# Padding TensorE's program with 95 small matmuls, and loading two rows of wo over ten DMA engines

## The chip, the cores and the metric

One core of a Trainium2 chip. Times are device microseconds of one execution of the whole kernel; a profile's span is a little shorter than the time (244.6 against 246.1 us for the kernel before). The ratios below compare fast runs of the same chip and the same rounds; e5 to e8 are single runs, taken for their traces, and their state is not known.

The names used below: PE is TensorE, the matrix engine; DVE copies and reduces; SyncE (SP) issues the loads; SBUF is the on-chip memory, which the kernel addresses as 128 partitions. The profile counts sixteen DMA engines; they carry a load in packets. A semaphore is a counter that the reader of the data waits on. The queues q1 and q8 are those of the big loads and of PE's program.

## The reference

Two attention layers decode one token each; their outputs are concatenated. Layer A looks at the last 2048 positions of its cache, B at all 8192.

```python
# B, S=1, D=576; Hq=32, Hkv=16, Sk=8192, Dh=128; all bfloat16
def ref(x, k_cache, v_cache, wq, wo, W):             # W = 2048 for A, 8192 for B
    q = (x @ wq).reshape(B, 1, Hq, Dh).transpose(0, 2, 1, 3)
    k = repeat(k_cache[:, :, Sk - W:], 2, axis=1)    # each kv head serves two query heads
    v = repeat(v_cache[:, :, Sk - W:], 2, axis=1)
    p = softmax(einsum("bhqd,bhkd->bhqk", q, k) * Dh ** -0.5)
    o = einsum("bhqk,bhkd->bhqd", p, v)
    return o.transpose(0, 2, 1, 3).reshape(B, 1, Hq * Dh) @ wo
```

The inputs that are read come to 102.76 MB, and each byte is used once.

## The kernel before

Each operation is recorded with what it reads and writes; semaphores and waits follow from that. All big loads are issued by SyncE into one region of SBUF called `slots`. A loop runs five times on TensorE (once for A, four times for B): transposes of K, scores, softmax, sums over V. Then comes wo. Partition p holds rows 32p to 32p + 31 of wo, so "row j" below means 128 rows of wo, one on each partition, 1152 bytes a partition.

```python
    def load(dst, src, writes, dma):
        add("sp", lambda sp: sp.dma_start(dst, src()), writes=writes, dma=dma)
    ...
    def load_wo(P, lo, n, off, res):
        load(slots[:, off:off + n * DM], lambda: wos[P].rearrange("(p j) n -> p (j n)", p=128)[:, lo * DM:(lo + n) * DM],
             res, "wo%d_%d" % (P, lo))

    def wo_part(P, lo, n, off, res):                 # four matmuls a row of B
        ...
    wo_loads = [                                     # layer, first row, rows, place, what must be free
        (0, 0, 32, 0, [("k", 0), ("k", 1, 0)]),
        (1, 0, 21, WQ_W, [("k", 1, 1)]),
        (1, 21, 7, 2 * SLOT, [("v", 0), ("v", 1)]),
        (1, 28, 3, 2 * SLOT + 7 * DM, [("w", 0)]),
        (1, 31, 1, 2 * SLOT + 10 * DM, [("w", 1)])]
    for P, lo, n, off, res in wo_loads:
        load_wo(P, lo, n, off, res)
    combine([NG - 1])                                # the attention output of the last group
    o_columns(1)
    for P in range(2):
        for Q, lo, n, off, res in wo_loads:
            if Q == P:
                wo_part(P, lo, n, off, res)
        finish_out(P)                                # copy, then the output's DMA
```

## Time and profile before

| | before |
|---|---|
| time | 246.02 us (245.89 to 246.11, 3 runs) |
| span of the profile | 244.6 us |
| loads on q1 | 102.76 MB, 98.1% of sixteen engines' span |
| fetches of PE's program (q8) | 6 packets of 16,384 bytes |
| last landing of wo of B, row 31 | 242.24 us |
| copy of the result starts | 242.59 us |

The page and the chain are shown in the prediction. Two readings need more than the page gives. A load over all 128 partitions steps its semaphore sixteen times (row 31 from 240.25 to 242.24 us). I take each step as one DMA engine's, so the sixteen times in the trace's semaphore records tell how far apart the engines are; "last" is what a waiting engine sees (row 31's last step at 242.24, PE's last four matmuls from 242.29). And each packet of a transfer has a start and a length. Packets follow end to start (most often the next one starts 3 or 4 ns before the recorded end), so in a busy stretch they can be chained into sixteen rows, which I take for the engines, with a few packets ambiguous where two rows meet. In the kernel before each of the sixteen rows has eight of the 128 packets of 24,192 bytes.

### The profile page before, as it was taken

Reading aid. Unit: us, or ns where it says so; the run is one execution under the profiler, and the core shown is the slowest. Engines: PE = TensorE matmul, PEld = TensorE weight load, DVE = VectorE, ACT = ScalarE, POOL = GpSimd, SP = SyncE. Lnnn points to the kernel's source line nnn. Section 1 sums busy time; section 2 is a strip of 40 time slices with the busy share of each in tenths; the row PEclk is TensorE's granted clock in tenths of the full one; section 3 lists DMA queues with packets and bytes.
Section 4 is the critical chain, followed back from the end, with each engine's and each line's share of the span. In section 5 each row is a group of like instructions: output and inputs, shape, how many; then the busy total and the mean of one; then the engine's idle time right before and its main releaser. Section 6 shows DMA issues by size and latency. Waiting matters only on the chain. (4 is left out here: it accounts for less than half of the span.)

```text
span 244.6 us, 5211 instructions
## 1 busy us (share of the span) xinstructions
PE 165.4 (68%) x2325; PEld 121.3 (50%) x2325; DVE 88.2 (36%) x152; ACT 92.7 (38%) x95; POOL 6.3 (3%) x33
## 2 busy tenths in 40 slices
PE   0007339968389995393999362999457799945965
PEld 0002139746236773233887221987232787624854
DVE  0001407864316454203556302455322246543031
ACT  2000016855306686102678300687600378630000
POOL 5000100000000000000000000000000000000000
PEclk9999957997759999569899859799957589975599
DMA  9999999999999999899999999999989999989993
GB/s 338 434 410 418 434 437 426 429 426 426 445 426 430 482 407 450 380 439 429 478 439 429 413 418 429 434 504 397 461 375 434 429 488 397 461 388 428 414 409 135
DMA packets 4068, 102.88 MB, mean 421 GB/s; under 512 B 602, under 2 KB 732, under 8 KB 988
## 3 DMA queue, kind: packets, MB, share of 16 engines
q1 hardware_dynamic: 3900, 102.76, 98.1%
q8 instruction: 6, 0.10, 0.2%
q10 hardware_dynamic: 160, 0.00, 0.0%
q14 instruction: 2, 0.02, 0.0%
HBM read 102.76 MB, written 0.00 MB: 420 GB/s over the span
## 5 line engine op out<-in xcount | busy, mean ns | idle before, releaser
L506 ACT ACTIVATE kt<-ktps 128x1024 bf16<-128x1024 bf16 x80 | 79.5, 1036 | 89.6 <-PE ktps L496 89.6
L496 PE MATMUL ktps<-ident,slots 128*128 128x128 bf16 x1280 | 87.8, 234 | 22.5 <-PEq L214 19.2
L496 PEld LDWEIGHTS ktps<-ident,slots 128*128 128x128 bf16 x1280 | 81.7, 106 | 38.0 <-issue 37.9
L509 DVE COPY kt<-ktps 128x1024 bf16<-128x1024 bf16 x80 | 60.7, 768 | 59.0 <-PE ktps L496 59.0
L588 PE MATMUL opsum<-slots,ptm 128*32 128x512 bf16 x320 | 28.5, 532 | 9.8 <-PEq L214 9.8
L521 PE MATMUL sacc<-kt,qst 128*32 128x512 bf16 x320 | 25.4, 392 | 2.2 <-PEq L214 2.2
L588 PEld LDWEIGHTS opsum<-slots,ptm 128*32 128x32 bf16 x320 | 14.0, 129 | 22.9 <-issue 20.6
L559 PE MATMUL misc<-ident,psb 128*128 128x128 bf16 x40 | 4.6, 285 | 15.8 <-PEq L214 15.8
L547 ACT ACTIVATE psb<-sacc,stat 128x2048 bf16<-128x2048 f32 x5 | 9.8, 1967 | 10.1 <-DVE stat L536 10.1
L606 DVE TENSOR_TENSOR vtmp<-opsum,maskV 128x512 f32<-128x512 f32 x4 | 2.8, 692 | 30.2 <-PE opsum L588 30.2
L559 PEld LDWEIGHTS misc<-ident,psb 128*128 128x128 bf16 x40 | 3.4, 125 | 18.2 <-issue 18.2
L438 PE MATMUL misc<-xnine,twice 64*128 64x18 bf16 x1 | 0.2, 170 | 18.0 <-DMA xnine<-in_B_x_dram 18.0
L566 DVE TENSOR_TENSOR ptm<-misc,maskP 128x1024 bf16<-128x1024 bf16 x5 | 3.5, 691 | 16.0 <-PE misc L559 16.0
L521 PEld LDWEIGHTS sacc<-kt,qst 128*32 128x32 bf16 x320 | 5.0, 94 | 8.3 <-issue 4.6
L438 PEld LDWEIGHTS misc<-xnine,twice 64*128 64x128 bf16 x1 | 0.1, 99 | 18.0 <-issue 18.0
L462 ACT ACTIVATE qrow<-opsum 128x512 bf16<-128x512 f32 x1 | 0.6, 597 | 19.4 <-PE opsum L456 19.4
L690 PE MATMUL ktps<-slots,opj 128*32 128x144 bf16 (+1 forms) x192 | 6.7, 247 | 0.7 <-issue 0.5
L690 PEld LDWEIGHTS ktps<-slots,opj 128*32 128x32 bf16 x192 | 5.3, 96 | 1.9 <-issue 0.6
L447 DVE TENSOR_SCALAR xpad<-misc,par 128x5 bf16<-128x5 f32 (+1 forms) x8 | 1.2, 229 | 13.8 <-PE misc L438 13.8
L481 POOL COPY qst<-qcol 128x32 bf16<-128x32 bf16 x8 | 1.7, 211 | 147.4 <-PE sacc L521 147.4
L559 PE MATMUL turned<-ident,psb 128*128 128x128 bf16 x40 | 5.3, 313 | 0.0
L534 DVE TENSOR_REDUCE stat<-sacc 128x1 f32<-128x512 f32 x5 | 3.5, 691 | 4.4 <-PE sacc L521 4.4
(75 smaller groups left out, 52.9 us busy)
## 6 DMA issues: line engine op xcount, KB each, us to landing
slots<-in_B_k_cache_dram SPq DMA_DIRECT2D x8, 4096.0 KB
slots<-in_A_k_cache_dram SPq DMA_DIRECT2D x4, 2048.0 KB
slots<-in_A_v_cache_dram SPq DMA_DIRECT2D x4, 2048.0 KB
slots<-in_A_wq_dram SPq DMA_DIRECT2D x1, 4608.0 KB, 13.8
slots<-in_B_wq_dram SPq DMA_DIRECT2D x1, 4608.0 KB, 24.0
slots<-in_A_wo_dram SPq DMA_DIRECT2D x1, 4608.0 KB, 18.7
slots<-in_B_wo_dram SPq DMA_DIRECT2D x1, 3024.0 KB, 25.5
slots<-in_B_wo_dram SPq DMA_DIRECT2D x1, 1008.0 KB, 7.7
```

Of the source, the lines that this page charges most:

```text
L481: return pool.tensor_copy(dst, src)
L496: ins = pe.matmul(ktps_bf[q][:, t * 128:(t + 1) * 128], lhsT=slots[:, o:o + 128], rhs=ident[:, :], start=True, stop=True, is_transpose=True)
L506: add("act", lambda act, src=src, dst=dst: act.activation(dst, src, ACT.Copy), reads=[("bank", q)], writes=[("kt", u % NKT, q)], tag="e%d% ...
L509: add("dve", lambda dve, src=src, dst=dst: dve.tensor_copy(dst, src), reads=[("bank", q)], writes=[("kt", u % NKT, q)], tag="e%d%d" % (u, q))
L521: ins = pe.matmul(sacc[32 * j:32 * j + 32, :], lhsT=qst[:, o:o + 32], rhs=rhs, start=(u == 0 and e == 0), stop=True, skip_group_check=True)
L534: add("dve", lambda dve: dve.tensor_reduce(st(C_M + g), sacc[:, :], AX.X, ALU.max), reads=[B_S], writes=[("st", C_M + g)], tag="max")
L547: return act.activation(dst, src, ACT.Exp, bias=st(C_NB + g), scale=SCALE, accum_out=st(C_L + g))
L559: ins = pe.matmul(dst[:, t * 128:(t + 1) * 128], lhsT=psb[:, o:o + 128], rhs=ident[:, :], start=True, stop=True, is_transpose=True)
L566: return dve.tensor_tensor(ptm[:, c * 1024:(c + 1) * 1024].rearrange("p (t y) -> p t y", t=8), dst.rearrange("p (t y) -> p t y", t=8), mas ...
L588: ins = pe.matmul(opsum[64 * j + 32 * x:64 * j + 32 * x + 32, :], lhsT=ptm[:, o:o + 32], rhs=v[:, at[0], at[1], :, :, b:b + 128], start=(n ...
L606: add("dve", lambda dve: dve.tensor_tensor(vtmp[:, :, :], src, by, ALU.mult), reads=[B_O, w], writes=["vtmp"], tag="keep")
L690: ins = pe.matmul(ktps[P][32 * j:32 * j + 32, 0:w], lhsT=opj[:, P, jj:jj + 32], rhs=slots[:, o:o + w], start=(jj == 0), stop=(jj == HQ - 1))
```

## The change

The intent, as I read the code: 95 small matmuls lengthen PE's program, from 1583 to 1773 instructions as built, and so move the places where it is fetched; and two rows of wo of B go over ten DMA engines (100 partitions over ten, 20 over ten, 8 over eight), so that the other six are spared, in the hope that these are the late ones.

```diff
+    def warm_up(n, after):
+        def mm(pe):
+            for k in range(n):
+                ins = pe.matmul(misc[0:32, 400:401], lhsT=ident[:, 0:32], rhs=ident[:, 0:1], start=True, stop=True)
+            return ins
+        add("pe", mm, reads=["ident"], writes=after)
+    warm_up(75, [B_M])                               # ahead of PE's first matmul
...
     def load_wo(P, lo, n, off, res):
-        load(slots[:, off:off + n * DM], ...)
+        cuts = [0, 100, 120, 128] if n == 2 else [0, 128]
+        def go(sp):
+            src = wos[P].rearrange("(p j) n -> p (j n)", p=128)
+            for a, b in zip(cuts, cuts[1:]):
+                ins = sp.dma_start(slots[a:b, off:off + n * DM], src[a:b, lo * DM:(lo + n) * DM])
+                if b < 128:
+                    op.also.append((16, ins))
+            return ins
+        op = add("sp", go, writes=res, dma="wo%d_%d" % (P, lo), inc=16 * (len(cuts) - 1))
...
-        (1, 21, 7, 2 * SLOT, [("v", 0), ("v", 1)]),
-        (1, 28, 3, 2 * SLOT + 7 * DM, [("w", 0)]),
+        (1, 21, 8, 2 * SLOT, [("v", 0), ("v", 1)]),
+        (1, 29, 2, 2 * SLOT + 8 * DM, [("w", 0)]),
...
+    warm_up(20, [B_M])                               # behind PE's last matmul
```

More of the change, by code (lines that the diff above doesn't have):

```diff
@@ L680, in load_wo @@
     def load_wo(P, lo, n, off, res):
-        load(slots[:, off:off + n * DM], lambda: wos[P].rearrange("(p j) n -> p (j n)", p=128)[:, lo * DM:(lo + n) * DM],
-             res, "wo%d_%d" % (P, lo))
+        cuts = [0, 100, 120, 128] if n == 2 else [0, 128]
[7 more added lines that the diff above has]
+        op = add("sp", go, writes=res, dma="wo%d_%d" % (P, lo), inc=16 * (len(cuts) - 1))
     def wo_part(P, lo, n, off, res):
```

## The prediction

The sum came to 245.7 us. Of its terms the time of the 75 matmuls stood as nothing, since they were to fit into 14 us of idle time.

Two things that the text uses are shown by runs. Multiples of 256 instructions, the "blocks": in e9, 512 instructions more bring eight packets of PE's program on q8 instead of six. Thirteen and twelve packets of 2304 bytes: in e2 eight chains have 13, two 12 and six none. The engines' numbers in the text, 0 to 15, are only names, and "the last six" are the six that carry no part of the two rows; no trace names an engine. That places are fixed or drift means that a fetch is carried by the same engine in every execution, or not.

> **What bounds the kernel now.** I read the page first: its slices and the DMA queues.
>
> ```profile
> PEclk9999957997759999569899859799957589975599
> DMA  9999999999999999899999999999989999989993
> ...
> q1 hardware_dynamic: 3900, 102.76, 98.1%
> q8 instruction: 6, 0.10, 0.2%
> ```
>
> The DMA row stays at 8 or 9 tenths until the last slice, and the loads of queue q1 alone fill 98.1% of sixteen engines' span, while PE, the next busiest, has 68% and idles whenever data is late. This kernel is a stream of 102.76 MB, and its time is when the last byte lands plus what must follow. The q8 line is small but matters: the program itself is fetched by the same engines, six times in the span (the trace has each as one packet of 16,384 bytes).
>
> Next, the chain of waits that ended last, from 228 us on:
>
> ```profile
> 228.10 5.04 PE opsum L588 x59
> ...
> 233.15 0.33 SPq L398
> ...
> 233.52 8.35 DMA slots<-in_B_wo_dram
> 241.87 0.04 issue
> 241.92 0.65 PE ktps L690 x16
> 242.56 0.02 issue
> 242.59 0.31 DVE outsb L698
> ```
>
> The end hangs on the landing of the last pieces of B's wo. Behind them come only 16 matmuls, a copy of 0.31 us and the output's own DMA (done at 244.6). The same stretch by windows:
>
> ```profile
> 238.00:239.00 1.00, 1.00 (x26) 0.84 (x24) 0.00 (x0) 0.00 (x0) 0.00 (x0) 1.00 0.97 391
> 239.00:240.00 1.00, 1.00 (x70) 0.98 (x68) 0.45 (x1) 0.00 (x0) 0.00 (x0) 1.00 0.94 362
> 240.00:241.00 1.00, 0.54 (x32) 0.35 (x24) 0.00 (x0) 0.00 (x0) 0.00 (x0) 1.00 0.45 175
> 241.00:242.00 1.00, 0.74 (x37) 0.56 (x41) 0.00 (x0) 0.00 (x0) 0.00 (x0) 1.00 0.16 59
> ```
>
> The last two numbers are the DMA share and GB/s. In the microsecond from 240 the share falls to 0.45, then 0.16: most engines are done and a few still drain. The trace's semaphore records show who. Every load steps its semaphore once for each engine. For the last row of wo (row 31) ten steps come from 240.25 to 240.94 us, the other six at 241.48, 241.68, 241.94, 241.98, 242.00 and 242.24. So **six engines trail by 1 to 2 us**. Early on nobody does: the steps of B's wq lie within 23.88 to 24.75. One step falls behind the rest after the fetch at 38.17 us, and more after those at 53.35, 62.28 and 70.21, until five trail by 229 us; a sixth joins after the fetch at 238.56. The packets' times can be chained end to start into sixteen rows, and the first four fetches lie in four different rows. Each occupied its engine for about 1.0 us (958 to 1073 ns a packet). No engine idles in this stream, so a delay of one is never made up: it shows at the end.
>
> PE around these landings, by the timeline:
>
> ```profile
> 240.98 0.68 PE L690 MATMUL ktps<-slots,opj 128*32 128x144 bf16 x30 [0.46 <-issue]
> 241.92 0.62 PE L690 MATMUL ktps<-slots,opj 128*32 128x144 bf16 x16 [0.26 <-DMA slots<-in_B_wo_dram]
> ```
>
> PE waits for rows 21 to 27 (last step 240.81, restart 240.98), runs 28 matmuls, waits for rows 28 to 30 (241.87), runs 12, waits for row 31 (242.24) and starts its last four at 242.29. The matmuls' starts are 62.5 ns apart for each row of four.
>
> [...]
>
> **The change, part by part.**
>
> *95 matmuls.* The built PE program grows from 1583 to 1773 instructions (95 x 2, a weight load and a matmul each). [...] The first 75 need only the identity (ready at 3.9 us) and stand before a matmul that starts at 18.0 us. [...] The last 20 follow PE's last useful matmul and run beside the copy and output DMA: free too. What they move is where blocks begin. With the instructions numbered as built, multiples of 256 are crossed before at 38.8, 46.8, 58.1, 71.0, 237.7 and 241.4 us: six crossings, six fetches, at roughly those times. Shifted by 150 instructions the crossings fall at about 25.1, 42.3, 49.8, 66.8, 108.4 and 239.4 us. So I expect no fewer fetches; the one of 238.56 comes near 108 instead, and the last near 240, now with loads perhaps still going. [...]
>
> *Rows of wo.* Before, each engine gets eight partitions of 7, 3 and 1 rows: packets of 8064, 3456 and 1152 bytes, from start to start 301, 131 and 47 ns. That is 8 x (301 + 131 + 47) = 3.83 us. After, 8 rows on all: by the slope between the first two, (301 - 131) / 4608 = 0.0369 ns per byte, a packet of 9216 bytes takes 344 ns, x8 = 2.75 us. Two rows in pieces of 100, 20 and 8 partitions: [...] so engines 0 to 7 take 10 + 2 + 1 = 13 packets of 2304 bytes and 8 and 9 take 12, at about 89 ns: 13 x 0.089 = 1.16 us. The last row: 8 x 0.047 = 0.38 us. Ten engines: 4.29 us, plus 0.46. Six engines: 3.13 us, minus 0.70. SyncE issues two DMAs more, at 0.33 us each, from 233.2 us; the 21-row load is in flight until 238.4, so this hides.
>
> *The sum, if the trailing six are the last six.* Rows 21 to 28 land at 240.81 + 8 x 0.043 = 241.15. Rows 29, 30 land on the ten at 240.58 (their latest for rows 28 to 30 before) + about 0.47 = 241.05. Row 31: the ten at 240.94 + 0.46 = 241.40, the six at 242.24 - 0.70 = 241.54. PE restarts at 241.15 + 0.17 = 241.32 and runs 11 rows without another wait; its last row starts 10 x 0.0625 later, at 241.95, against 242.29. **Gain 0.34 us**, less than the 0.70 taken from the six, because PE's 11 rows behind the bigger 8-row load become the bound. Span 244.6 - 0.34 = 244.25; time 246.02 - 0.34 = 245.7 us.
>
> **Rivals.**
> 1. *The trailing engines are others than 10 to 15, or drift between executions.* Then a trailing engine gets the 13 packets instead of none: row 31 at 242.24 + 0.46 = 242.70, time 246.5. For it: no engine is named in this trace. [...]
> 2. *[...] nothing is fetched any more.* Then nobody trails, and the ten loaded engines are last: row 31 at 241.40, PE's last four at 241.45, time 246.02 - 0.84 = 245.2. [...]
> 3. *The late fetch near 240 us hits a loaded engine*, costing it 1.0 us: row 31 at about 241.40 + 1.0 = 242.4, time about 246.1. Most engines are done by then, so I give it little.
> 4. *PE's early matmuls or shifted clock windows slow a stage.* PE is not the bound before 240 us, so 0.
>
> **Range and chances.** I weight the main sum at about 0.65, rivals 1 and 3 at 0.25 together, rival 2 at 0.1. Before's three runs spread over 0.22 us. Prediction 245.7, range 245.1 to 246.4. The largest of all effects here is 0.84 us, 0.34% of the time, so a change of over 2% (4.9 us) has no mechanism: 0.01 each way.
>
> **What would show it.** After: six packets on q8 in the span, near 25, 42, 50, 67, 108 and 240 us; a few packets of 2304 bytes (128) on ten engines; the semaphore of row 31 with its sixteen steps drawn together to about 0.3 to 1.0 us instead of 2.0; the DMA share from 240 us on higher and then ending sooner, near 0 after 241.3; PE with one wait before its last 44 matmuls (for the 8-row load), not three. A row-31 spread that stays at 2 us with the last step near 242.7 is rival 1; no q8 packets is rival 2. What would make it wrong is chiefly a wrong guess of which engines carry the fetches.

## The result, and the profile after

The changed kernel takes **247.28 us** (247.17 to 247.53, six runs) against 245.99 us: ratio 1.0054, 95% interval 1.0041 to 1.0067, so 1.3 us slower. (A ratio is the mean time of one kernel's runs over that of the other's of the same rounds, so not quite the ratio of the medians.) Against the predicted 245.7 us, range 245.1 to 246.4, it is outside and on the other side.

From the page of the kernel after:

```profile
DMA  9999999999999999999999999999999999999993
...
q1 hardware_dynamic: 3912, 102.76, 98.0%
q8 instruction: 7, 0.11, 0.2%
```

The stream is as full as before. The windows of its end (the last two numbers are the DMA share and GB/s):

```profile
238.00:239.00 1.00, 0.66 (x44) 0.66 (x48) 0.00 (x0) 0.00 (x0) 0.00 (x0) 1.00 1.05 417
239.00:240.00 1.00, 0.83 (x56) 0.64 (x44) 0.00 (x0) 0.00 (x0) 0.00 (x0) 1.00 1.04 258
240.00:241.00 1.00, 0.00 (x0) 0.00 (x0) 0.00 (x0) 0.00 (x0) 0.00 (x0) 1.00 0.86 205
241.00:242.00 1.00, 0.00 (x0) 0.00 (x0) 0.00 (x0) 0.00 (x0) 0.00 (x0) 1.00 0.48 134
```

Before, from 239 to 240 us the engines were 94% busy and moved 362 GB/s. Now they are busy throughout (1.04; a packet counts whole in the window where it starts) and move 258. Busy engines with fewer bytes mean longer packets. The chain and PE's timeline of the kernel after:

```profile
232.46 10.61 DMA slots<-in_B_wo_dram
243.07 0.04 issue
243.12 0.55 PE ktps L709 x10
243.66 0.51 PE misc L438 x19
```

```profile
242.11 0.69 PE L709 MATMUL ktps<-slots,opj 128*32 128x144 bf16 x32 [2.27 <-DMA slots<-in_B_wo_dram]
243.12 0.55 PE L709 MATMUL ktps<-slots,opj 128*32 128x144 bf16 x12 [0.32 <-DMA slots<-in_B_wo_dram]
243.72 0.31 DVE L717 CAST outsb<-ktps 128x144 bf16<-128x144 f32 x1 [5.87 <-PE ktps L709]
```

PE waits twice for wo: for rows 21 to 28 until 242.06, where I had 241.15, and for rows 29 and 30 until 243.07, where I had 241.05. The copy starts at 243.72, 1.13 us later than before, as much as the spans of the two profiles differ (245.7 against 244.6 us). The chain ends in the padding (L438) only because it follows the last instruction: the copy starts 0.05 us after the last useful matmul, as before, so it does not wait for the padding. The packets of the tail, by size, in ns (trace of each kernel):

```
                     bytes   count   shortest  median  mean  longest
before                8064    128      305       305    306    312
                      3456    128      135       135    139    371
                      1152    128       51        51     51     53
after                 9216    128      347       351    392    713
                      2304    128       93       148    141    255
                      1152    128       51        63     65    116
```

Before, nearly all packets of one size take the same time; the three long ones of 3456 bytes overlap the fetch at 238.56. After, 100 of 128 packets of 2304 bytes take over a tenth longer than the shortest, and the stretching reaches the packets of the other loads.

### The profile page after: what moved, and what is told of

The parts are those of the page before. It is cut to its first block, busy times and chain, and to the rows that moved or that the text cites. A ratio compares the mean times of both kernels' runs of the same rounds, so it can differ in the third digit from the quotient of the medians.

```text
span 245.7 us, 5403 instructions
## 1 busy us (share of the span) xinstructions
PE 166.4 (68%) x2420; PEld 121.7 (50%) x2420; DVE 88.1 (36%) x152; ACT 92.2 (38%) x95; POOL 6.3 (3%) x33
## 5 line engine op out<-in xcount | busy, mean ns | idle before, releaser
L506 PE MATMUL ktps<-ident,slots 128*128 128x128 bf16 x1280 | 85.9, 231 | 19.2 <-PEq L214 19.2
L506 PEld LDWEIGHTS ktps<-ident,slots 128*128 128x128 bf16 x1280 | 79.9, 104 | 34.6 <-issue 34.6
L598 PE MATMUL opsum<-slots,ptm 128*32 128x512 bf16 x320 | 28.5, 532 | 9.7 <-PEq L214 9.7
L438 PE MATMUL misc<-ident 128*32 128x1 bf16 x95 | 2.9, 166 | 4.0 <-POOL ident L383 4.0
```

The source lines that it names most:

```text
L438: ins = pe.matmul(misc[0:32, 400:401], lhsT=ident[:, 0:32], rhs=ident[:, 0:1], start=True, stop=True)
L506: ins = pe.matmul(ktps_bf[q][:, t * 128:(t + 1) * 128], lhsT=slots[:, o:o + 128], rhs=ident[:, :], start=True, stop=True, is_transpose=True)
L598: ins = pe.matmul(opsum[64 * j + 32 * x:64 * j + 32 * x + 32, :], lhsT=ptm[:, o:o + 32], rhs=v[:, at[0], at[1], :, :, b:b + 128], start=(n ...
```

## The experiments

**The theory.** It is my guess, and no record in a trace names what it rests on: engines that write to neighbouring partitions at one time hold each other up. A load over all 128 partitions pairs engines and partitions in one way, eight packets to each of sixteen rows; a piece of 100 partitions over ten engines pairs them otherwise. Moreover, the bytes for a late engine's partitions would be held up whoever carries them, so that sparing the engine does not help. The expectations call this the "port theory". **Rivals**: the padding's shifted fetches; the larger first piece (8 rows, not 7); trailing engines that are among the ten after all.

**e1, the padding alone.**

```diff
-        (1, 21, 8, ...), (1, 29, 2, ...)     # of the changed kernel
+        (1, 21, 7, ...), (1, 28, 3, ...)     # so no piece has two rows, and none is cut
```

> The padding alone (95 matmuls), wo of B loaded as before in 7, 3 and 1 rows on all engines. Port theory[...]: the padding costs nothing, 246.0 us, ratio 0.998 to 1.002; seven q8 packets. Padding theory (its shifted instruction fetches cause the loss): about 247.3 us.

Measured 246.25 us (six runs) against 246.09: ratio 1.0017, interval 1.0004 to 1.0031. That is inside what I wrote, but the interval excludes 1: about 0.4 us slower on average. Four of the six runs lie at 246.19 to 246.30, two at 246.86 and 247.15; no trace of these two is kept, so their cause stays open. In any case this is not the whole loss. All packets of 1152 and 3456 bytes stay near 51 and 135 ns. The q8 line reads otherwise than I expected, six and not seven:

```profile
q8 instruction: 6, 0.10, 0.2%
```

They start at 28.58, 43.82, 58.73, 70.26, 76.54 and 239.85 us; the seventh of the kernel after (244.23) belongs to the very end, and this span ends without it.

**e2, the ten-engine loads alone.** The changed kernel without its two calls of `warm_up`.

> The loads of 8, 2 and 1 rows with the two rows on ten engines, no padding. Port theory: 247.0 to 247.6 us; packets of 2304 bytes take about 140 ns on average against 93 alone, and the slowest packets of 9216 bytes over 500 ns against 347. Padding theory: 246.0 us. Wrong-engine theory (the loss comes only from trailing engines that are among the ten): later or earlier by luck, packets at 93 and 347 ns.

Measured 247.34 us, ratio 1.0050 (1.0037 to 1.0063): the whole loss without the padding. Eight chains have 13 packets of 2304 bytes, two have 12, six none. Packets of 2304 bytes have mean 123 ns (I had said about 140), the longest of 9216 bytes is 868 ns. (That one lies beside a fetch, as does one of 849 ns in e3 below; without it the longest are 548 to 572, still over the 500 that I expected.) The windows of e2:

```profile
238.00:239.00 1.00, 0.53 (x36) 0.54 (x40) 0.44 (x1) 0.00 (x0) 0.00 (x0) 1.00 0.95 384
239.00:240.00 1.00, 0.96 (x62) 0.77 (x50) 0.00 (x0) 0.00 (x0) 0.00 (x0) 1.00 0.93 249
240.00:241.00 1.00, 0.24 (x2) 0.10 (x2) 0.00 (x0) 0.00 (x0) 0.00 (x0) 1.00 0.68 178
```

The drop from 384 to 249 GB/s at a share of 0.93 is that of the kernel after. So the padding is not needed for the loss, and the padding theory falls.

**e3, the resizing alone.**

```diff
-        cuts = [0, 100, 120, 128] if n == 2 else [0, 128]     # of e2
+        cuts = [0, 128]
```

> Loads of 8, 2 and 1 rows, each over all sixteen engines, no padding: the resizing alone. Port theory: packets of 2304 bytes at 93 ns, of 9216 at 347 ns; time 246.0 to 246.3 us (rows 21 to 28 land 0.34 us later, PE then runs 11 rows). If the larger first piece were the loss: about 247 us.

Measured 246.14 us, ratio 1.0002 (0.9989 to 1.0015). Packets of 2304 bytes: median 93, mean 94, longest 102 ns. Windows and PE's timeline of e3:

```profile
239.00:240.00 1.00, 0.75 (x49) 0.56 (x36) 0.00 (x0) 0.00 (x0) 0.00 (x0) 1.00 0.95 374
240.00:241.00 1.00, 0.00 (x0) 0.00 (x0) 0.00 (x0) 0.00 (x0) 0.00 (x0) 1.00 0.49 174
```

```profile
241.07 1.31 PE L708 MATMUL ktps<-slots,opj 128*32 128x144 bf16 x44 [1.32 <-DMA slots<-in_B_wo_dram]
```

The same pieces over all sixteen engines move 374 GB/s, and rows 21 to 28 land at 241.02, close to my 241.15. So the 8-row piece was sized right, and the loss of e2 comes from how the two rows are spread.

**e4, same engines' bytes, other destinations.**

```diff
-        cuts = [0, 100, 120, 128] if n == 2 else [0, 128]     # of e2
+        cuts = [0, 64, 128] if n == 2 else [0, 128]
```

> As e3, but the two rows go as partitions 0 to 63 and then 64 to 127, both over sixteen engines, so every engine carries the same bytes as in e3 and only the destinations differ[...]. Port theory: packets of 2304 bytes at 120 to 190 ns, time 0.3 to 0.7 us over e3. If only the uneven load of the engines or the small number of engines mattered: packets at 93 ns and the time of e3.

Measured 247.00 us, ratio 1.0031 (1.0018 to 1.0044), by the medians 0.86 us over e3: more than I had said. Packets of 2304 bytes: median 98, mean 122, longest 260 ns. Windows and PE's timeline of e4:

```profile
239.00:240.00 1.00, 1.00 (x76) 1.00 (x68) 0.00 (x0) 0.00 (x0) 0.00 (x0) 1.00 1.08 262
```

```profile
242.26 0.69 PE L708 MATMUL ktps<-slots,opj 128*32 128x144 bf16 x32 [2.02 <-DMA slots<-in_B_wo_dram]
243.25 0.55 PE L708 MATMUL ktps<-slots,opj 128*32 128x144 bf16 x12 [0.31 <-DMA slots<-in_B_wo_dram]
```

The engines are busy throughout (share 1.08, in e3 0.95), yet they move 262 GB/s and not 374. I built the halves to go over sixteen engines each; the landings of e4 are not on record, but in the kernel before the two loads of x, over 64 partitions, step their semaphores sixteen times. If the halves do so too, neither a small number of engines nor uneven load is needed for the loss, and which engine carries which partitions, and when, is enough. Every byte has the same source and the same destination as in e3; what differs is that each transfer reaches only one half of the partitions.

Two rivals remain for e4. *Two transfers instead of one*: a trace speaks against it. In the kernel before, A's cache comes in eight transfers over all partitions, queued one behind the other, and 1021 of their 1024 packets are within a tenth of the shortest. *The source*: with the partitions, the rows of wo in HBM that are read at one time change too. Whole loads don't mind how far apart the sources of their partitions lie (packets of 16,384 to 65,536 bytes, from caches and weights laid out differently, all take 0.037 ns a byte in the kernel before), but no run here separates source from destination.

**e5, destinations by themselves.** Behind the end of the kernel before, SyncE issues four sets of four loads, each set after the one before has landed; they overwrite memory that is no longer used.

```diff
+    probe("whole", 0, 1, 128)      # first partition, step, count; 8064 bytes each
+    probe("spread", 64, 4, 8)
+    probe("packed", 120, 1, 8)
+    probe("low32", 0, 1, 32)
```

> The kernel before with four sets of extra loads after its end, alone on the chip's queues, all in packets of 8064 bytes (305 ns in the stream): 128 partitions; 8 partitions 4 apart (64, 68, ... 92[...]); 8 adjacent partitions (120 to 127[...]); 32 adjacent partitions (0 to 31[...]). [...] If only the number of engines mattered[...]: 8 spread and 8 adjacent alike. If neither: 305 ns in all four.

The theory's figures for the four sets, 305, 305, 1220 and 610 ns, were worked out from a layout of the memory that no run shows.

The packets, in ns:

```
set      partitions            median   mean   note
whole    0 to 127                305     324
spread   64, 68, ... 92          439     433    302 to 580
packed   120 to 127              761     802    the last sixteen: 839 to 1235, median 1167
low32    0 to 31                 620     558
```

Eight adjacent partitions are not like eight spread ones: 761 against 439 ns. In the second half of the packed set a packet takes about 1167 ns. If the eight packets of a load run side by side, that is 8 x 8064 bytes in 1167 ns, by this estimate 55 GB/s in all, while the shortest packets move 8064 bytes in 302 ns, 26.7 GB/s each. The set's first sixteen packets took only 319 to 682 ns; a limit of the destinations alone doesn't explain this start. The set of 32 takes twice as long as the whole one (620 against 305 ns). My figure for the spread set, 305, was wrong: 433. Something besides adjacent destinations holds those loads up, and no run shows what.

**e6, e7, e8: which engines trail?** The changed kernel twice more, and e2's once more, unchanged. A chain with packets of 2304 bytes belongs to one of the ten engines, one without to the six spared (in e2 ten chains and six).

> The changed kernel once more, for which engines trail: by the 21-row load five or six engines trail. [...] again all but one of the trailing ones carry no packet of 2304 bytes; if places drift, another number. Time 247.3 us and packets of 2304 bytes at about 140 ns either way.

> The ten-engine loads without padding once more. In e2 four of the five engines that trailed before the tail carried packets of 2304 bytes. If places drift[...], another number here; if they are fixed, again four of five. Time 247.3 us in either case by the port theory; the wrong-engine theory has it move by up to 0.5 us with the number.

> The changed kernel a third time, as e6: fixed places give the same trailing engines in the same roles, drifting ones do not.

Times 247.29, 247.34 and 247.14 us (one run each). With padding, six engines trail at the end of the 21-row load. In e6 the chains separate cleanly: five of the six carry no packet of 2304 bytes and one does. The first profile and e8 agree, apart from one ambiguous chain in each. Without padding five trail there, and four of them carry such packets, in e2 and in e7 alike. So the padding did move the late engines into the spared six, all but one. The reason that I gave for the padding, that without it the places drift, did not show: e2 and e7 agree. The times don't depend on how many of the ten are late (ratios 1.0054 with one, 1.0050 with four), but that does not refute the wrong-engine theory, since one late engine among the ten is enough to delay the last landing. What it can't explain is the stretched packets and the size: by the prediction's own sum such an engine costs 0.46 us, not 1.3, and e4, built so that all engines carry the same, still loses 0.86.

What sparing bought the five can be read off: from the end of the 21-row load to the end of row 31 on the trailing chains.

```
                        21-row load ends    row 31 ends        apart
e6, the five spared     237.64 to 237.93    241.71 to 242.14   4.06 to 4.22 us
e3, the five trailing   237.51 to 237.78    241.39 to 241.65   3.87 to 3.88 us
```

An engine in e3 carries eight packets of 2304 bytes more, and still needs less time: 3.88 us on average against 4.11. In e6 the five were rid of that work (8 x 0.089 = 0.71 us) and got it back with interest: their packets of 9216 bytes average 453 to 486 ns, against 348 or 349 in e3. Over the traces with the ten-engine pieces, the mean packet of 2304 bytes takes 119 to 141 ns instead of 94 (e3), and of the neighbours' 9216 bytes 383 to 392 instead of 353.

**e9, does a fetch make an engine trail?**

```diff
+    warm_up(256, [B_M])     # 512 instructions, two blocks, ahead of PE's first matmul; nothing else
```

> The kernel before with 256 tiny matmuls (512 instructions, two blocks) ahead of PE's first matmul and nothing else, so all later block starts fall on the same code as before. If a fetched block is what makes an engine trail: two more q8 packets, between 4 and 20 us, and two more engines behind by about 1 us already at the landing of B's wq near 24 us, where before all sixteen steps lie within 0.87 us; at the 21-row load seven or eight trail. Time 246.0 to 246.4 us. If trailing has another cause: the steps near 24 us stay within 0.9 us.

The q8 line of e9:

```profile
q8 instruction: 8, 0.13, 0.2%
```

The two more start at 10.28 and 16.87 us. The last four of the sixteen steps at the landing of B's wq, and the steps at the 21-row load:

```
before  wq of B      ... 24.41 24.50 24.52 24.75
e9      wq of B      ... 24.63 24.64 25.57 25.88
before  rows 0-20    ... 236.91 237.09 | 237.63 237.82 238.10 238.14 238.40
e9      rows 0-20    ... 236.94 236.99 | 237.77 237.93 237.94 238.18 238.21 238.22 238.25
```

Two engines more are behind by about 1 us from the two fetches on, and seven trail in the end, not five. The time does not move (246.02 us, ratio 1.0004, 0.9987 to 1.0020): the last landing depends on the latest engine, not on how many are late. PE also stood for 2.58 us between two tiny matmuls after 223 of them, beside the fetch at 10.28 us; that it waited for the fetch is likely, not shown.

One late engine is left over: before, four fetches of q8 come ahead of 229 us, but five engines trail. The fifth falls behind between the landings at 74.91 and 84.61 us, where the page's other queue of kind "instruction", q14, has a packet of 8192 bytes (at 78.76 us). In e3 and e9 too an engine more trails after that queue's packet near 78 or 79 us. I overlooked this in the prediction, and no run tests it.

## Why the prediction was wrong

*What bounds the kernel, and why engines trail.* Right. The stream and its last landing set the end in every run, and e9 shows that a fetch of PE's program puts an engine behind. I had no fetch for one of the five late engines; the record points to q14 (see e9).

*Cost of the 95 matmuls: nothing.* Nearly right: e1 is at 1.0017 (1.0004 to 1.0031), so a small cost, about 0.4 us, is likely, and its cause is open. My estimate for the first 75 was too long: they took 2.16 us in e1. Nothing hung on it.

*The fetches.* I had six, near 25, 42, 50, 67, 108 and 240 us. They came at 28.5, 47.1, 58.5, 68.9, 76.4 and 239.6, and a seventh at 244.2. The one I put at 108 came at 76.4 probably because the loop's closing instructions lie behind the piece that A's pass skips, so that already this pass enters the block; I read this from the program, and no run tests it.

*"If the trailing six are the last six."* Five of the six were; one was among the ten. Rival 1 needs only one such engine, so in part it came true: its sign was a row-31 spread that stays at 2 us, and the steps lie from 241.02 to 243.29. But its sum ends at 242.70, so it doesn't cover the loss either.

*The step that failed is "13 x 0.089 = 1.16 us", and with it the 344 ns of the 8-row packets.* I took packet times from loads over all 128 partitions and used them for pieces that pair engines and partitions otherwise. Measured means are 141 ns for 2304 bytes, and about 450 ns for the 9216 bytes of the trailing engines (averages of 443 to 458 a chain in the first profile). That makes 8 x (0.450 - 0.344) = 0.85 us for rows 21 to 28, which landed at 242.06 instead of 241.15. Behind this alone PE's last row would start at 242.11 + 10 x 0.0625 = 242.73, 0.44 us later than before's 242.29, where I had a gain of 0.34: the stretched packets turn the gain into a loss even with the spared engines. The rest came from the one trailing engine that is among the ten. It ended its 9216-byte packets, stretched to 443 ns on average, at 241.1, then had 13 of 2304 bytes until 242.46, and its step for rows 29 and 30, at 243.07, released PE. The granted clock was 0.50 by then (0.12 us a row instead of 0.0625), and the same engine's step for row 31 came at 243.29; the last row started at 243.34. That is 0.44 + 0.61 = 1.05 of the 1.13 us; the rest is the last matmuls themselves, 324 to 328 ns long instead of 237 or 238.

*Behind it, the idea that load can be taken off a late engine.* "Minus 0.70" for the six was not wrong as a count of their own bytes, but they were no quicker for it: from the 21-row load to the end of row 31 they needed 4.11 us in e6, against 3.88 in e3. That is measured. The reason that I give, that the bytes for those partitions were held up whoever carried them, is argued: e4 and the second half of e5's packed set fit it, e5's spread set and the start of the packed one don't follow from it, and the source in HBM was not varied by itself. No record in the trace names what a packet waits for.

*Rival 3* happened in the first profile as a smaller part: the fetch at 239.61 met one of the ten, whose row 31 stepped at 242.89, earlier than the trailing engine's 243.07 and 243.29 that counted. *Rival 2* did not happen. *One wait for PE* was wrong: two, for the reason above.

No version here beats the kernel before: e3 and e9 are level with it.

## What to carry to other kernels

In a full stream of loads, ask which partitions the bytes go to, not only which engine carries them: here pieces that paired engines with partitions otherwise than a whole 128-partition load lost more (0.86 us in e4, 1.3 in the change) than was meant to be gained (0.34). Carry packet times over only between loads with the same pairing. When the DMA share stays near 1 and the GB/s fall, look at the packet lengths first.
